# New constants for a planner's transfer model, and a new table of due times, in a planned linear-attention and MLP-mixer kernel

## The chip, the cores and the metric

The kernel runs on one core of one Trainium2 chip. The metric is the device time of one execution in microseconds (us); for the kernel before it is given as the median of three runs. A profile is one further execution, recorded by the hardware profiler. TensorE is written PE, VectorE DVE, ScalarE ACT, GpSimd POOL, and SyncE SP.

## The reference, cut to what matters

Two branches start from the same normalised rows; one gates the other, and the input is added. S is 2048 rows, D is 512, F is 1376, and attention has 32 heads of 16.

```
x  = A_x
xn = layernorm(x)
s  = A(xn)                    # linear attention
g  = silu(B(xn))              # mixer and MLP
return x + s * g

A: q, k, v = split(xn @ wqkv); phi(t) = where(t > 0, t + 1, exp(t)) + 1e-6
   kv = sum_s phi(k) v^T;  z = sum_s phi(k)
   o  = phi(q) kv / (phi(q) z + 1e-6);  A = o @ wo
B: h  = gelu(layernorm(xn) @ w1); its four column groups shifted by +1, -1, +2, -2 rows
   x1 = xn + shifted(h) @ w2
   B  = x1 + gelu(layernorm(x1) @ w3) @ w4
```

## The kernel before, in words

The rows are cut into 16 tiles of 128, four to a block, so that there are four blocks of 512 rows. Each product is made from rounded halves (names ending in `h` and `l`): three matmuls stand for one exact one. The work runs in this order: keys and queries of the four blocks with the running Gram sums (`k`, `q`, `pax`, `pbx`, `pex`, `g`), the first mixer product (`h`), the second (`pam`, `pbm`, `pem`), the up-projection (`a`, `pa`, `pb`, `pe`) with attention between its parts (`pas`, `pbs`, `pes`), and the down-projection (`acc` for block 0, `pad`, `pbd`, `ped` for blocks 2, 3 and 1).

No instruction is issued where the program text names it. The text builds a list of 5542 operations (`Plan.add`, with a duration, the tiles read and written and, for a transfer, its megabytes `mb`). `Plan.emit` then goes through simulated time: it picks the next operation of each engine, gives it its buffers and issues it. What it picks is set by

- the due time of each operation: matmuls get theirs from a nominal sequence (`deadlines`), all others one that leads back from what they feed (`backward`);
- the table `SOONER`, pairs of an operation's number and a whole number k: `nudged` moves that operation's due time earlier by 0.25 us times k (later where k is negative), and then carries the change back to what feeds it;
- the simulated time at which its inputs are there and its buffers are free. For PE an operation may be taken out of turn only when its nominal place lies at most 9 us behind that of the first one not yet done (`window=9.0`).

Transfers are simulated as one queue, `dma`, the time at which the last transfer leaves it. Ordinary transfers (loads, stores and fetches) are issued from SP; adding transfers (`gather`, the form in which the transfer adds to what lies in SBUF) are issued from POOL, `soft` in the code. At most eight of each kind are simulated as under way (`under`). For a transfer issued at time `s`, `op.end` is the simulated time of landing, from which its readers and the free buffers are counted. Each engine runs what it was given in the order of issue, and semaphores guard the data, so a wrong estimate costs waiting and nothing else.

The places that the prediction speaks of: a block's rows are read and their statistics made (`load_rows`, `totals`); `spread(b)` makes from them four numbers per row, which PE turns, ACT copies (`ar`) and SP stores to two rows in HBM (`arow`, `nrow`); `load_u(b, 1)` loads the transposed input in four parts (`xt`, 128x512 f32, 0.262 MB each) and adds the row `nrow` to each by an adding transfer; each part is then rounded by ACT (`u_ch`) and its rest made by DVE (`u_cl`), and these feed the products of `pair_kq`. `phi_k` adds each key tile to `zacc` by an adding transfer, `mix2` adds the normalised rows (`o<-xnd`), `gate` adds the input (`th<-in_x`).

Of the kernel before, what the change touches and what calls it, by code (L numbers as in the profile page):

```python
# [85 lines left out]
class Plan:  # L86
# [183 lines left out]
    def emit(self, first, lead, reserve, window, ahead, table=()):  # L270
# [13 lines left out]
        port, dma = 0.0, 0.8  # L284
# [6 lines left out]
        while left:  # L291
# [5 lines left out]
            for e, cands in avail.items():  # L297
                picks = []
                low = INF
                for op in cands:  # L300
                    s = max(free[e], op.ready)
                    if op.mb:
                        s = max(s, under[e == "POOL"][0] + self.GAP)
                    if op.two and s < port:
                        s = port
                    if e == "POOL" and not op.mb and not op.two:
                        s = next((b + .02 for a, b in lock if a <= s < b), s)
                    if op.table is not None and op.table != table:
                        s = max(s, free[e] + 1.28)
                    ok = True  # L310
                    fresh = [t for t in op.tiles if t.ap is None]
                    for t in fresh:
# [7 lines left out]
                        s = max(s, q[need - 1][0] + (self.GAP if e != "PE" else self.PE_GAP))  # L320
# [24 lines left out]
            s, op = best  # L345
# [13 lines left out]
            op.end = s + op.lat * k  # L359
            if op.mb:  # L360
                soft = e == "POOL"
                late = min(.92, 1.03 * max(0.0, dma - s))
                dma = max(dma, s + (.97 if soft else .06)) + op.mb * (4.59 if soft else 3.43)
                op.end = max(dma + (1.89 if soft else 1.29) + late, s + (4.08 if soft else 2.08 if op.loads else 2.2))
                under[soft].pop(0)
                under[soft].append(op.end)
            if op.two:
# [29 lines left out]
def linear_attn_gated_by_mixer(  # L397
# [1398 lines left out]
    for b in LINE:  # L1796
# [9 lines left out]
        down_late(b, final)  # L1806

    SOONER = (
# [48 lines left out]
    )  # L1857
    pl.emit(first=6.0, lead={"p": 9.0, "w": 20.0, "ab": 10.0}, reserve={"p": 8, "w": 1, "ab": 0}, window=9.0,
            ahead=6.0, table=SOONER)
# [39 lines left out]
```

## Time and profile before

| | us |
|---|---|
| median of 3 runs (lowest, highest) | 503.36 (502.1, 504.45) |
| the profiled execution, its own time | 506.13 |
| its span, first to last instruction's end | 504.4 |
| PE busy | 495.1 |
| DVE busy | 436.9 |
| ACT busy | 370.6 |
| POOL busy | 124.1 |

The page of the profile gives busy time by engine, shares in 40 slices, the queues of the transfers, and the chain of work that ended last. Other views answer for a part: waits (which engine waited for whose instruction), a table by stretches of time (busy time of each engine with the number of its instructions, the granted clock of PE, the share of the transfer engines that was busy and the GB/s), one tile's instructions, and the chain of waits in order of time. A busy time of PE is taken from start to modelled end, and matmuls overlap; the number of matmuls in a stretch tells more than its busy time.

### The profile page before, as it was taken

How to read it: one execution, taken by the hardware profiler on the slowest of the kernel's cores; microseconds unless marked ns; L12 is line 12 of the kernel's file. 1: busy time of each engine (PE TensorE's matmuls, PEld its weight loads, DVE VectorE, ACT ScalarE, POOL GpSimd, SP SyncE). 2: the span in 40 equal slices, each digit the busy share in tenths (PEclk: the TensorE clock that was granted, in tenths of full speed). 3: DMA queues.
4: the chain of work that ended last, by engine and by line, in shares of the span. 5: the costliest groups of instructions: out<-in, count | busy, mean ns of one | idle time of the engine just before them, and what ended most of it. 6: DMA issues, size and time to landing. Idle time of an engine off the chain costs nothing.

```text
span 504.4 us, 9873 instructions
## 1 busy us (share of the span) xinstructions
PE 495.1 (98%) x3240; PEld 446.8 (89%) x3240; DVE 436.9 (87%) x869; ACT 370.6 (73%) x840; POOL 124.1 (25%) x214
## 2 busy tenths in 40 slices
PE   8999979999999999999999999999999999999996
PEld 5788857777788988799988989999999999999996
DVE  4998768699889967999899999999999789795973
ACT  5897979976768669999996757765676676664631
POOL 1384601717950213042210021100000000144330
PEclk9999999999999999999999999999999999999999
DMA  7869895799994699979985789986443789689996
GB/s 218 304 168 230 218 261 139 177 280 275 301 324 102 181 282 305 293 206 259 344 278 196 231 187 265 254 278 185 145 126 106 239 277 329 175 163 291 297 249 177
DMA packets 87083, 117.44 MB, mean 233 GB/s; under 512 B 10328, under 2 KB 39160, under 8 KB 87032
## 3 DMA queue, kind: packets, MB, share of 16 engines
q1 hardware_dynamic: 75512, 96.11, 58.4%
q0 software_dynamic: 11520, 20.71, 24.1%
q8 instruction: 25, 0.41, 0.4%
q14 instruction: 26, 0.21, 0.1%
HBM read 72.66 MB, written 39.93 MB: 223 GB/s over the span
## 4 chain that ended last, share of the span: by engine, by line
PE 89%; DMA 5%; DVE 3%; ACT 2%; SPq 1%; issue 0%; DVEq 0%; ACTq 0%
PE pb L146 9%; PE pbd L146 9%; PE h L146 9%; PE g L146 8%; PE acc L146 6%; PE pbx L146 5%; PE pe L146 5%; PE pbm L146 5%; PE ped L146 5%; PE pbs L146 4%; PE q L146 3%; PE k L146 3%; PE pex L146 3%; PE pad L146 3%; PE pem L146 2%; PE pa L146 2%
## 5 line engine op out<-in xcount | busy, mean ns | idle before, releaser
L225 POOL DMA_DIRECT2D xo<-x1d x12 | 10.8, 948 | 160.5 <-ACT d_a11xh L168 110.9
L225 POOL DMA_DIRECT2D o<-xnd x16 | 14.0, 894 | 48.9 <-ACT o L168 19.1
L225 POOL DMA_DIRECT2D th<-in_x x14 | 12.3, 905 | 38.4 <-DVE th L201 23.2
L225 POOL DMA_DIRECT2D zacc<-ke x12 | 11.9, 991 | 31.6 <-DVE xf L191 21.8
L168 ACT ACTIVATE th<-xo 128x512 f32<-128x512 f32 (+1 forms) x16 | 9.5, 611 | 11.4 <-DVE xo L201 10.1
L225 POOL DMA_DIRECT2D xt<-nrow x16 | 14.9, 1373 | 7.4 <-DMA nrow<-ar 4.2
L168 ACT ACTIVATE ht<-ht 128x512 f32<-128x512 f32 x16 | 9.8, 626 | 6.7 <-DVE ht L191 6.7
L191 DVE TENSOR_TENSOR ht<-h,abc 128x512 f32<-128x512 f32 x16 | 10.9, 685 | 4.4 <-PE h L146 4.0
L168 ACT ACTIVATE p<-pb 128x256 f32<-128x256 f32 x20 | 7.6, 382 | 9.1 <-PE pb L146 8.9
L196 POOL TENSOR_SCALAR w<-mv 128x4 f32<-128x4 f32 (+2 forms) x10 | 4.4, 440 | 36.0 <-ACT sq L168 35.6
L168 ACT ACTIVATE y<-o,nm,rs 128x512 f32<-128x512 f32 x16 | 12.0, 806 | 0.5 <-POOL nm L196 0.5
L168 ACT ACTIVATE sq<-o,mv 128x512 f32<-128x512 f32 x16 | 11.5, 721 | 0.1
L168 ACT ACTIVATE p<-pe 128x256 f32<-128x256 f32 x20 | 7.7, 383 | 5.2 <-PE pe L146 4.8
L201 DVE SCALAR_TENSOR_TENSOR pq<-pq,rd 128x512 f32<-128x512 f32 x16 | 10.8, 680 | 0.2
L201 DVE SCALAR_TENSOR_TENSOR qz<-pq,zb 128x512 f32<-128x512 f32 x16 | 10.8, 679 | 0.0
L1456 DVE TENSOR_REDUCE den<-qz 128x32 f32<-128x512 f32 x16 | 10.7, 679 | 0.1
L598 POOL TENSOR_TENSOR rs<-w,nhalf 128x4 f32<-128x4 f32 (+2 forms) x10 | 10.2, 1020 | 0.7
L168 ACT ACTIVATE sq<-o 128x512 f32<-128x512 f32 x16 | 9.9, 625 | 0.0
L168 ACT ACTIVATE u<-pb 128x256 f32<-128x256 f32 x20 | 7.7, 383 | 3.1 <-PE pb L146 2.8
L168 ACT ACTIVATE x<-x,nm,rs 128x512 f32<-128x512 f32 x12 | 9.0, 805 | 0.0
L201 DVE SCALAR_TENSOR_TENSOR th<-th,so 128x512 f32<-128x512 f32 x12 | 8.1, 680 | 0.6 <-ACT th L168 0.5
L168 ACT ACTIVATE sq<-x,mv 128x512 f32<-128x512 f32 x12 | 8.5, 710 | 0.0
(2043 smaller groups left out, 2435.2 us busy)
## 6 DMA issues: line engine op xcount, KB each, us to landing
w_s<-in_w SPq DMA_DIRECT2D x28, 256.0 KB
x<-in_x SPq DMA_DIRECT2D x16, 256.0 KB
xt<-in_xt SPq DMA_DIRECT2D x16, 256.0 KB
xnd<-x SPq DMA_DIRECT2D x16, 256.0 KB
xt<-nrow POOLq DMA_DIRECT2D x16, 256.0 KB, 7.9
pqd<-qr SPq DMA_DIRECT2D x16, 256.0 KB
o<-xnd POOLq DMA_DIRECT2D x16, 256.0 KB, 7.1
x1d<-o SPq DMA_DIRECT2D x16, 256.0 KB
```

Of the source, the lines that this page charges most:

```text
L146: lambda: nc.tensor.matmul(out.get(), lhs.get(), rhs.get(), start=start, stop=stop, skip_group_check=more))
L168: nc.scalar.activation(out.get(), src.get(), func, scale=get(scale), **kw)
L191: self.vec(eng, out, [a, b], lambda: self.e(eng).tensor_tensor(out.get(), a.get(), b.get(), op=op), True)
L196: lambda: self.e(eng).tensor_scalar(out.get(), a.get(), get(s1), get(s2), **kw), False,
L201: lambda: self.nc.vector.scalar_tensor_tensor(out.get(), a.get(), get(s), b.get(), op0=op0, op1=op1),
L225: lambda: self.nc.gpsimd.dma_start(out.get(), get(src), accum_op=ALU.add), mb=mb)
L598: lambda: g.tensor_tensor(out.get(), src.get(), nh.get(), op=ALU.pow))
L1456: pl.add("DVE", .6, .68, [t], [den], lambda: nc.vector.tensor_reduce(den.get(), t.get().rearrange("p (h d) -> p h d", d=DH), axis=AX.X, op ...
```

## The change

The list of operations, their sizes, tiles and dependences stay as they are. Changed are the constants by which `Plan.emit` simulates a transfer, and the whole table `SOONER`. In the simulation an ordinary transfer takes 2.92 us per MB instead of 3.43, an adding one 4.93 instead of 4.59; the time from issue to entering the queue, from leaving it to landing, and the shortest time from issue to landing change as well, and the part of the delay `late` that grows with the queue grows by half. A load and a store no longer differ in their shortest time. The old table has 490 pairs, the new one 565; 197 operations stand in both, 56 of them with the same number.

```diff
             if op.mb:
                 soft = e == "POOL"
-                late = min(.92, 1.03 * max(0.0, dma - s))
-                dma = max(dma, s + (.97 if soft else .06)) + op.mb * (4.59 if soft else 3.43)
-                op.end = max(dma + (1.89 if soft else 1.29) + late, s + (4.08 if soft else 2.08 if op.loads else 2.2))
+                late = min(1.38, 1.54 * max(0.0, dma - s))
+                dma = max(dma, s + (.66 if soft else .39)) + op.mb * (4.93 if soft else 2.92)
+                op.end = max(dma + (2.12 if soft else 1.46) + late, s + (3.02 if soft else 2.21))
                 under[soft].pop(0)
                 under[soft].append(op.end)
...
     SOONER = (
-        23, 8, 39, 7, 48, -50, 69, 53, 90, 10, 93, 21, 96, 20, 97, 12, 99, 9, 106, -6, 118, -9, 120, 6, 124, 8,
...
-        -29, 5428, -15, 5478, -18, 5486, -12, 5493, 8, 5514, 38, 5519, -24,
+        23, 13, 37, 5, 41, 2, 47, -18, 48, -112, 52, -101, 54, 3, 60, 2, 72, 7, 92, -38, 95, -17, 96, 48, 100,
...
+        5373, -5, 5379, 30, 5380, -25, 5392, 17, 5419, 19, 5422, -29, 5478, -30, 5493, 13, 5513, 18,
     )
```

99 rows, old and new, of the table SOONER are left out of this document.

## The prediction, made before the result was known

> **What bounds the kernel now.** I read the page first, for what is busy.
>
> ```profile
> span 504.4 us, 9873 instructions
> ## 1 busy us (share of the span) xinstructions
> PE 495.1 (98%) x3240; PEld 446.8 (89%) x3240; DVE 436.9 (87%) x869; ACT 370.6 (73%) x840; POOL 124.1 (25%) x214
> ```
>
> PE is busy for 98% of the span, but matmuls overlap in these records, so I went on to the table by stretches, which counts them. Columns: stretch, its length, then busy us and (number) of PE, weight loads, DVE, ACT and POOL, then PE's granted clock, the busy share of the transfer engines, GB/s.
>
> ```profile
> 60.00:65.00 5.00, 5.00 (x24) 4.03 (x23) 4.40 (x8) 5.00 (x10) 3.37 (x4) 1.00 0.90 236
> 65.00:70.00 5.00, 5.00 (x23) 4.09 (x22) 3.19 (x6) 3.45 (x6) 0.00 (x0) 1.00 1.11 204
> 70.00:75.00 5.00, 2.21 (x7) 1.20 (x7) 2.95 (x8) 3.06 (x6) 0.00 (x0) 0.93 1.02 327
> 75.00:80.00 5.00, 5.00 (x18) 3.97 (x17) 4.13 (x8) 4.10 (x8) 0.87 (x1) 0.73 0.74 179
> 80.00:90.00 10.00, 10.00 (x44) 8.00 (x44) 7.22 (x12) 10.00 (x26) 2.58 (x5) 1.00 0.44 129
> 80.00:180.00 100.00, 100.00 (x470) 81.46 (x470) 88.50 (x168) 77.80 (x154) 43.81 (x95) 1.00 0.82 225
> 180.00:300.00 120.00, 120.00 (x800) 108.90 (x799) 108.56 (x220) 102.58 (x254) 23.09 (x34) 1.00 0.91 259
> 300.00:500.00 200.00, 199.65 (x1674) 198.63 (x1673) 175.21 (x362) 124.86 (x301) 25.18 (x29) 1.00 0.80 223
> 500.00:504.40 4.40, 0.40 (x4) 0.19 (x2) 1.54 (x3) 0.38 (x1) 0.00 (x0) 0.99 0.45 165
> ```
>
> From 80 to 500 us PE is idle for 420 - (100.00 + 120.00 + 199.65) = 0.35 us. An order can give nothing back there; it can only lose. Between 70 and 80 us stand 7 + 18 = 25 matmuls where a steady ten microseconds hold 44: 19 are missing, and at 10/44 = 0.227 us each that is **4.3 us lost**. The waits of PE name the cause (columns: who waited for whom, us in total, times, the longest):
>
> ```profile
> PE pax L146 <- DVE u_2l L191: 2.3, 1, 2.3
> PE warm L146 <- POOL ones L514: 1.0, 1, 1.0
> PE k L146 <- ACT u_1h L168: 0.8, 1, 0.8
> PE pax L146 <- ACT u_2h L168: 0.5, 1, 0.5
> PE k L146 <- DVE wk_1l L191: 0.3, 1, 0.3
> ```
>
> The pair of projections that opens block 2 waits for the third part of its input, 0.5 us for the half `u_2h` and 2.3 us for `u_2l`: 2.8 us. The other 4.3 - 2.8 = 1.5 us are a slower clock behind the wait:
>
> ```profile
> 72.00:74.00 2.00, 0.00 (x0) 0.00 (x0) 1.53 (x4) 1.03 (x2) 0.00 (x0) 1.00 1.05 387
> 74.00:76.00 2.00, 1.78 (x4) 1.48 (x5) 2.00 (x6) 1.82 (x5) 0.87 (x1) 0.57 0.50 191
> 76.00:78.00 2.00, 2.00 (x7) 1.52 (x6) 2.00 (x5) 1.70 (x4) 0.00 (x0) 0.58 0.78 137
> ```
>
> From 74 to 78 us 11 matmuls ran at a granted 0.57 and 0.58, where 4/0.227 = 17.6 would fit: 6.6 x 0.227 = 1.5 us, as the remainder says. The view of the tile `xt` in 50 to 80 us shows why the data were late (times of the first and last start stand behind the durations):
>
> ```profile
> L225 POOL DMA_DIRECT2D xt<-nrow x4: 864/1387/1711, 58.9 to 60.8; - x4
> L168 ACT ACTIVATE u_0h<-xt x1: 615/615/615, 66.5 to 66.5; 128x512 fp32r<-128x512 f32 x1
> L168 ACT ACTIVATE u_3h<-xt x1: 630/630/630, 72.5 to 72.5; 128x512 fp32r<-128x512 f32 x1
> DMA to landing us min/median/max: 6.8/9.5/11.7
> ```
>
> Four adding transfers are issued between 58.9 and 60.8 us; the reader of the first starts at 66.5, that of the last at 72.5. They land (72.5 - 66.5)/3 = 2.0 us apart, the slowest 11.7 us after its issue.
>
> **The change part by part.** *The operations.* Nothing is added or removed: the same 3240 matmul records, the same transfers. Cost 0. What the constants cost on the chip is 0 too; they act through the order alone.
>
> *How well the new constants fit.* The queues, with their share of the 16 transfer engines over the span:
>
> ```profile
> q1 hardware_dynamic: 75512, 96.11, 58.4%
> q0 software_dynamic: 11520, 20.71, 24.1%
> ```
>
> Ordinary: 0.584 x 504.4 / 96.11 = 3.06 us per MB; the old 3.43 is 12% too slow, the new 2.92 5% too fast. Adding: 0.241 x 504.4 / 20.71 = 5.87; the old 4.59 is 22% too fast, the new 4.93 16%. Both move towards the trace. That speaks for a truer plan, with one warning: the side of the error for ordinary transfers changes, from cushion to shortage.
>
> *The stall of block 2.* With the issue times of before, the simulated landing of the last `xt` part moves by: 0.262 MB x (4.93 - 4.59) = 0.09 us for each adding transfer, 0.45 for four and the `zacc` one among them; 2.12 - 1.89 = 0.23 behind the queue; at most 1.38 - 0.92 = 0.46 of `late`; 0.66 - 0.97 = -0.31 ahead of it. The sum is +0.8 us. So the new plan sees a gap of 0.262 x 4.93 = 1.29 us between two adding transfers instead of 1.20, where the trace has 2.0. It has a reason to bring this chain forward by 0.8 us, not by the whole wait of 2.8. Bounds: 0, if the new order leaves the chain where it is, and 2.8, if it happens to be early enough. I take 0.8, which the constants give. PE cannot fill much of the hole with later work: it may reach only 9 us ahead, and a pair is 42 matmuls, 9.5 us. What is late next is the fourth part, one gap of 2.0 us behind the third and read by the same product.
>
> *The clock behind it.* A wait of 2.0 us in place of 2.8 leaves the 1.5 us somewhere between all paid and none. Nothing here shows a wait of that length, so 0 to 1.5 saved; I take 0.5, nearer to the one row there is. The Trainium skill ("TensorE: Matmul & The Clock Gate", "What's actually happening") says that the clock halves after an idle window of about 3.4 us. The trace disagrees in the length: here it fell to 0.57 after a longest wait of 2.3 us. By the rule a shortened wait would cost no clock at all and the saving would be 0.8 + 1.5 = 2.3 us, which would be 501.1.
>
> *The start.* The first waits, 1.0, 0.8 and 0.3 us, follow the first loads and constants. The table touches early operations (47, 48 and 52 make the key weights' halves), so up to 2.1 us can go and about as much can come. I take 0, since nothing queues ahead of the first loads.
>
> *80 to 500 us.* 0 to gain. I take 0, and what can be lost is the second rival.
>
> *The end.* The chain of waits ends so (start, us, what):
>
> ```profile
> 498.14 2.27 PE pbd L146 x19
> 500.44 0.39 ACT th L168
> 500.86 0.44 DVE th L201
> 501.31 0.42 DVE th L191
> ```
>
> Behind the last matmul are three operations and one store, 504.4 - 500.4 = 4.0 us. The order of these is forced by data; another store just ahead would cost 0.262 x 3.06 = 0.8 us, or save it. I take 0.
>
> **The sum:** -0.8 - 0.5 = -1.3 us. The profiled execution took 506.13 us for its span of 504.4 and lies 2.77 us above the median of 503.36; its span would become 503.1 and its time 504.8. From the median: 503.36 - 1.3 = **502.1 us**.
>
> **The rivals.** *The stall goes altogether.* The whole order in front of it is made anew, with 75 pairs more in the table, and the chain of statistics, `nrow`, `xt` and `u` has many places to win two microseconds: the store of `nrow` alone kept POOL waiting 4.2 us.
>
> ```profile
> POOL xt L225 <- DMA nrow<-ar: 4.2, 1, 4.2
> ```
>
> Against it: the constants ask for 0.8 only. It gives 503.36 - 4.3 = 499.1.
>
> *A new wait in the late stages, slower.* The chain of waits runs through stores and fetches where PE does not stop yet, and one stage is full of ordinary transfers:
>
> ```profile
> 399.97 2.05 DMA wf_b211h<-w4d
> 405.67 6.43 DMA wt<-wt_40h
> 400.00:425.00 25.00, 24.90 (x210) 24.68 (x209) 23.00 (x48) 18.66 (x44) 0.00 (x0) 1.00 0.90 291
> ```
>
> In these 25 us 291 GB/s are 7.28 MB. The old plan counts 25.0 us for them, the new one 21.2, the trace has 0.90 x 25 = 22.5. A plan that holds the queue to be 3.7 us shorter may issue fetches that much later or put other transfers ahead; if the cushion was all there was, PE waits 3.7 us and pays the 1.5 us of slow clock. That is +5.2, and with the forecast's -1.3 it gives 503.36 + 3.9 = 507.3. It decides once a fetch or the store of 6.43 us lands later than PE needs it by over 1.3 + 2.5 = 3.8 us, clock included. For it: PE idles 0.10 us there already. Against it: the old 11% of cushion is spread over many transfers, and DVE and ACT have idle time to catch up.
>
> *The change does not do what it says.* If adding and ordinary transfers share the engines, no single queue with fixed rates says when one lands, and the stall stays, perhaps at another place: 503.4, between 501.5 and 505.5. The row for 65 to 70 us speaks for it: share 1.11 and only 204 GB/s, against 387 GB/s at 1.05 in 72 to 74. The Trainium skill ("DMA: Bandwidth & Descriptors", "Queues, rings and completion order") says that each transfer engine goes round between the queues that have work, a packet at a time. By that rule an adding transfer is slowed by ordinary ones issued after it, which this plan cannot count; the gap of 2.0 us against its 1.29 agrees.
>
> **How the numbers follow.** The forecast, a stall that is shortened, has a chance of 0.33; the stall gone 0.32; the new wait 0.29; the case in which the change does not do what it says 0.06. About 0.5% (2.5 us) is what a measurement here tells from no change. The forecast and the third rival are within it: 0.39 together. The stall gone is faster by more: 0.32. The new wait is slower: 0.29. The forecast's own range is 501.1 to 503.4, from the clock fully saved to no gain. For 8 in 10: the low end is 499.1 less 0.6 of the start's 2.1, 498.5; the high end 507.3 and a store's 0.8 at the end, 508.1.
>
> **What the profile of after would show.** The table by stretches: the stretch with fewer than 44 matmuls in 10 us, between 65 and 85; 21 missing or more means no gain, under 5 the first rival. The waits of PE: `pax` for `u_2l`, near 1.5 us by the forecast. A wait of PE over 1 us for a `wf`, `wu`, `yt` or `d_` tile after 180 us, and a granted clock below 0.9 behind it, is the second rival. It would be wrong in its ground if PE's matmul counts between 80 and 180, 180 and 300 or 300 and 500 us changed by over 10 with no wait named, or if the time outside the span moved by over 1 us.

## The result, and the profile after

The changed kernel takes 508.05 us (median of 9 executions, 506.06 to 509.75) against 503.36 us for the kernel before (median of 9, 501.08 to 506.47): a ratio of 1.0071, 95% interval 1.0045 to 1.0097. It is slower, by about 0.7% in this comparison. The unaltered pair was run side by side twice more: 507.16 against 505.90 (1.0013, 0.9991 to 1.0036) and 506.69 against 504.76 (1.0041, 1.0012 to 1.0070). All three ratios lie over 1, two of them clear of 1; the loss is small, some 0.4% or 2 us, and single executions scatter by more than that. The intervals of the first two do not even meet, so ratios of different sets of runs that lie half a per cent apart say little. So below an edit is judged first by the stretch of the profile that it touches, and only then by its time.

The profiled execution of the changed kernel took 509.00 us for a span of 507.0; the time outside the span went from 1.7 to 2.0 us, which is 0.3 us of the loss. From the page of the changed kernel:

```profile
span 507.0 us, 9889 instructions
...
PE 494.8 (98%) x3240; PEld 445.2 (88%) x3240; DVE 436.3 (86%) x869; ACT 372.2 (73%) x840; POOL 127.9 (25%) x214
...
q1 hardware_dynamic: 75512, 96.11, 58.3%
q0 software_dynamic: 11520, 20.71, 24.3%
```

The work is the same: the same transfers, bytes and matmul records. The table by stretches, first one row of the kernel before, then the changed kernel (columns as in the prediction):

```profile
70.00:80.00 10.00, 7.21 (x23) 5.16 (x23) 7.09 (x15) 7.16 (x13) 0.87 (x1) 0.83 0.88 253
```

```profile
70.00:80.00 10.00, 10.00 (x44) 7.72 (x43) 9.16 (x19) 9.17 (x17) 0.86 (x1) 1.00 1.07 340
80.00:180.00 100.00, 99.98 (x473) 81.82 (x471) 87.68 (x166) 76.50 (x151) 44.05 (x94) 1.00 0.82 224
180.00:300.00 120.00, 120.00 (x806) 109.20 (x805) 109.18 (x220) 103.18 (x254) 23.12 (x35) 1.00 0.88 251
300.00:500.00 200.00, 196.02 (x1640) 194.65 (x1640) 172.08 (x356) 123.65 (x297) 24.69 (x28) 1.00 0.82 225
```

The stall of block 2 is gone: 44 matmuls between 70 and 80 us where there were 23, and no slow clock. But from 300 to 500 us there are 1640 instead of 1674. The waits of PE say where new holes are:

```profile
PE pb L146 <- ACT u L168: 2.4, 2, 1.2
PE ab L151 <- POOL an L196: 2.0, 1, 2.0
PE ped L146 <- DVE d_s11l L191: 1.6, 1, 1.6
PE warm L146 <- POOL ones L514: 1.1, 1, 1.1
```

To place them, the same stretches of both kernels, first the kernel before, then the changed one:

```profile
30.00:40.00 10.00, 10.00 (x45) 7.98 (x44) 9.18 (x16) 7.75 (x17) 9.43 (x13) 1.00 0.84 201
310.00:330.00 20.00, 20.00 (x171) 20.00 (x171) 19.90 (x43) 15.16 (x40) 1.72 (x2) 1.00 0.97 280
470.00:480.00 10.00, 10.00 (x87) 10.00 (x86) 9.74 (x19) 6.83 (x14) 4.37 (x5) 1.00 1.10 294
```

```profile
30.00:40.00 10.00, 7.97 (x35) 6.14 (x34) 7.98 (x13) 6.45 (x12) 9.58 (x12) 1.00 0.59 150
310.00:330.00 20.00, 17.59 (x143) 16.90 (x142) 16.82 (x37) 11.97 (x33) 1.75 (x2) 1.00 0.98 249
470.00:480.00 10.00, 8.43 (x72) 8.22 (x71) 7.97 (x16) 6.79 (x14) 3.53 (x4) 1.00 1.05 263
```

Counted in matmuls at the rate of the full rows: 21 more in block 2 at 10/44 us are 4.8 us won; 10 fewer at 30 to 40 us are 2.3 lost; 28 fewer at 310 to 330, at 20/171 us, are 3.3 lost; 15 fewer at 470 to 480, at 10/87, are 1.7 lost. The balance of these four is a loss of 2.5 us; the spans differ by 2.6. That they agree so well is in part luck, since smaller differences remain: 5 fewer in the rest of 20 to 60 us, 9 more from 180 to 300, 15 more from 330 to 470. The rows from 0 to 300 us, of the kernel before and of the changed one, show that the changed kernel is still ahead there, by 13 matmuls, in spite of the hole at 34 us:

```profile
0.00:300.00 300.00, 295.07 (x1566) 247.94 (x1567) 260.15 (x505) 245.32 (x539) 98.91 (x185) 0.99 0.86 240
```

```profile
0.00:300.00 300.00, 295.78 (x1579) 247.84 (x1580) 260.81 (x507) 247.17 (x542) 103.17 (x186) 1.00 0.85 239
```

What decides is behind 300 us. How each hole comes about:

*At 34 us.* PE's transposition `ab` of block 1 waits for POOL's small operations on the statistics. Their rows in the kernel before and in the changed one (start, us, engine, what):

```profile
29.57 0.53 POOL L196 TENSOR_SCALAR pu<-mv 128x4 f32<-128x4 f32 x1 [0.62 <-DVE mv L587]
30.19 1.37 POOL L598 TENSOR_TENSOR an<-pu,nhalf 128x4 f32<-128x4 f32 x1
```

```profile
29.53 3.39 POOL L196 TENSOR_SCALAR pu<-mv 128x4 f32<-128x4 f32 x1 [0.49 <-DVE mv L587]
33.01 1.48 POOL L598 TENSOR_TENSOR an<-pu,nhalf 128x4 f32<-128x4 f32 x1
```

The same 128x4 operation starts at the same time and takes 3.39 us instead of 0.53. Beside it DVE runs a train of operations that read two operands in SBUF, each starting before the one ahead has ended:

```profile
29.77 0.69 DVE L191 TENSOR_TENSOR x1l<-x,x1h 128x512 fp32r<-128x512 f32 x1
30.38 1.29 DVE L201 SCALAR_TENSOR_TENSOR kr<-kt,kr 128x512 f32<-128x512 f32 x2
31.58 0.69 DVE L191 TENSOR_TENSOR x2l<-x,x2h 128x512 fp32r<-128x512 f32 x1
32.18 0.69 DVE L191 TENSOR_TENSOR kq_f<-wk_s,wq_s 128x512 f32<-128x512 f32 x1
32.91 0.69 DVE L201 SCALAR_TENSOR_TENSOR kq_f<-kq_f,wq_s 128x512 f32<-128x512 f32 x1
```

The last one reads what the fourth writes and starts only when that is through (32.18 + 0.69 = 32.87); POOL's operation ends at 29.53 + 3.39 = 32.92, just there. The hole belongs to the new table: with it and the old constants (e8) PE waits 2.4 us for `ab`, with the old table and the new constants (e11) 0.6.

*At 316 and 323 us.* ACT takes its work in order, and ahead of the copies `u` that PE needs stand the rounding of `q4t` and the copy of `q5t`. Both wait for a fetch:

```profile
316.56 0.63 ACT L168 ACTIVATE q4h<-q4t 128x512 fp32r<-128x512 f32 x1 [2.91 <-DMA q4t<-q4d]
...
323.83 0.42 ACT L168 ACTIVATE q<-q5t 128x256 fp32r<-128x256 f32 x1 [2.11 <-DMA q5t<-q5d]
```

In the kernel before `q4h` ran at 316.30 with no wait. The four fetches of `q4t` (64 KB each) were issued from 307.5 to 310.2 us. The trace shows the landing of the first two, at 315.9 and 316.1, 8.4 and 8.0 us after their issue.

If I put the issue times of the trace into the new constants, the four land at 312.4 to 312.9, over 3 us too early. The old constants give 312.5 to 313.0, nearly the same. So at this place the exchange of the constants did not make the estimate worse. From 300 to 350 us the kernel before has 422 matmuls and the changed kernel 390; the new table with the old constants (e8) has 396, the old table with the new constants (e11) 409. By these single profiles most of this loss comes with the new table.

*At 477 us.* ACT's `d_s21h` waits until an output store gives its buffer back, and holds `d_s11h` behind it:

```profile
474.15 0.63 ACT L168 ACTIVATE d_s21h<-d1f_s21f 128x512 fp32r<-128x512 f32 x1 [2.63 <-DMA out<-th]
```

### The profile page after: what moved, and what is told of

Same layout as the page of the kernel before. It is cut to its first block, busy times and chain, and to the rows that moved or that the text cites. A ratio compares the mean times of both kernels' runs of the same rounds, so it can differ in the third digit from the quotient of the medians.

```text
span 507.0 us, 9889 instructions
## 1 busy us (share of the span) xinstructions
PE 494.8 (98%) x3240; PEld 445.2 (88%) x3240; DVE 436.3 (86%) x869; ACT 372.2 (73%) x840; POOL 127.9 (25%) x214
## 3 DMA queue, kind: packets, MB, share of 16 engines
q1 hardware_dynamic: 75512, 96.11, 58.3%
## 4 chain that ended last, share of the span: by engine, by line
PE 81%; DMA 9%; DVE 4%; ACT 2%; POOL 1%; SPq 1%; issue 1%; DVEq 0%; ACTq 0%
PE pb L146 10%; PE h L146 9%; PE pbd L146 7%; PE g L146 7%; PE acc L146 6%; PE pbx L146 6%; PE pe L146 5%; PE pbm L146 4%; PE pbs L146 4%; DMA out<-th 4%; PE ped L146 3%; PE pex L146 3%; PE pa L146 3%; PE pem L146 2%; PE a L146 2%; PE pes L146 2%
## 5 line engine op out<-in xcount | busy, mean ns | idle before, releaser
L201 DVE SCALAR_TENSOR_TENSOR qr<-qe,qi 128x512 f32<-128x512 f32 x11 | 7.5, 685 | 1.8 <-ACT qe L168 1.8
```

The costliest lines, as they stand in the source:

```text
L201: lambda: self.nc.vector.scalar_tensor_tensor(out.get(), a.get(), get(s), b.get(), op0=op0, op1=op1),
```

## The experiments

Theory A: the loss is the sum of these few waits, each made by an operation that stands in an in-order queue behind something that comes later than the planner counts. Rival B: the waits only show what was late first, and time saved at one of them is waited out at the next. Further rivals are named with their runs. "Ratio" is to the kernel before in the same set of runs (its medians were 505.42, 505.90, 504.85, 504.28 and 504.76 us in the five sets, in the order of time).

| run | us | ratio, 95% interval |
|---|---|---|
| e1_q4_behind | 508.13 | 1.0053 (1.0023, 1.0083) |
| e2_pu_on_dve | 506.04 | 1.0011 (0.9988, 1.0034) |
| e3_late_store | 506.90 | 1.0037 (1.0010, 1.0063) |
| e4_all_three | 505.94 | 1.0014 (0.9987, 1.0042) |
| e5_after_again | 507.16 | 1.0013 (0.9991, 1.0036) |
| e6_gaps_in_dve | 506.42 | 1.0024 (0.9994, 1.0055) |
| e7_no_adding_at_306 | 504.88 | 0.9983 (0.9958, 1.0009) |
| e8_new_table_old_constants | 510.22 | 1.0084 (1.0055, 1.0113) |
| e9_fetch_by_due | 506.90 | 1.0044 (1.0018, 1.0071) |
| e10_gaps_fetch_store | 506.16 | 1.0018 (0.9999, 1.0038) |
| e11_old_table_new_constants | 508.63 | 1.0090 (1.0064, 1.0115) |
| e12_before_again | 506.92 | one execution |
| e13_adding_after_fetch | 507.28 | 1.0054 (1.0019, 1.0090) |
| e14_after_third | 509.00 | 1.0088 (1.0053, 1.0122) |
| e15_no_table_old_constants | 515.22 | 1.0193 (1.0137, 1.0249) |
| e16_no_table_new_constants | 520.06 | 1.0312 (1.0242, 1.0383) |
| e17_after_once_more | 506.69 | 1.0041 (1.0012, 1.0070) |
| e18_no_table_ordinary_new | 517.61 | 1.0259 (1.0194, 1.0324) |

### The unaltered kernels again: e5, e17, e12

> The changed kernel once more, unaltered, as the base for the runs beside it. Theory A (its new waits belong to its order, not to one execution): the profile shows again about 2 us for the transpose ab behind POOL, 2 to 3 us for u in the stretch of 310 to 330 us, 1 to 2 us for the operands of ped, and no wait for pax; 0.4 to 1.0% slower than the kernel before. Rival (the losses of the first profile were of that execution): other waits in other places, and a ratio whose interval holds 1.

> The unaltered changed kernel beside the unaltered kernel before, a third time. Theory A (the change is a loss of some 0.4%, the mean of the two comparisons so far): ratio 1.002 to 1.007. Rival H (the first comparison was an outlier, there is no difference): ratio 0.998 to 1.002.

> The kernel before, unaltered, for a second profile of its stall in block 2. Theory A (the stall belongs to its order): again a wait for pax of 2 to 3 us between 70 and 80 us, 22 to 30 matmuls in that stretch, and a clock under 0.7 behind it. Rival G (the first profile of before, at 506.13 us against a median of 503.36, fell on an execution with a long stall, and it varies): a wait of less than 1.5 us there and over 36 matmuls.

In both new profiles of the changed kernel PE waits 2.0 us for `ab`, and 2.4 and 2.2 us for `u`; between 310 and 330 us it is busy 17.59 and 17.77 us, as in the first (17.59). Those two belong to the order. The wait for `d_s11l` does not: 0.2 us in e5, none in e17. The kernel before shows its stall again, shorter, with a wait of 1.8 us for `u_2l`:

```profile
70.00:80.00 10.00, 8.21 (x29) 5.93 (x28) 7.53 (x16) 7.98 (x14) 0.86 (x1) 0.83 1.00 276
```

With 29 matmuls it loses 15 x 10/44 = 3.4 us there. Both profiles of the kernel before (506.13 and 506.92 us) are of executions above its medians, so what the stall costs in a usual one is not shown. Of the two ratios one lies in the interval of theory A and one in that of rival H; the three together speak for about 0.4%.

### The hole at 34 us: e2 and e6

e2 gives `pu<-mv` of block 1 to DVE, at its place in the order:

```diff
         pl.ts(p, var(mv1, b * QT, b * QT + QT), kv * (1.0 + EPS), EPS * EPS, ALU.mult, ALU.add, eng="POOL")
+        if b == 1:
+            v = var(mv1, b * QT, b * QT + QT)
+            pl.ops[-1].emit = lambda: nc.vector.tensor_scalar(
+                p.get(), v.get(), kv * (1.0 + EPS), EPS * EPS, op0=ALU.mult, op1=ALU.add)
```

> The changed kernel, but the small operation pu<-mv of block 1 (128x4, 3.39 us on POOL in the profile after, 0.53 in the profile before) is given to DVE at the same place of the order; nothing else is moved. Theory A: the wait of PE for the transpose ab (2.2 us lost at 32.4) goes for the most part, since the power behind it still runs on POOL; the time falls by 1.2 to 2.2 us, to about 506.3. Rival B: the power operation or the other POOL operations of the group are stretched beside DVE instead, or the next operand is late, and the time falls by less than 0.6 us.

The wait for `ab` stays at 1.6 us. POOL's next operation is stretched instead, from 1.48 us to

```profile
30.37 3.20 POOL L598 TENSOR_TENSOR an<-pu,nhalf 128x4 f32<-128x4 f32 x1 [1.59 <-DVE pu L624]
```

So it is the place that stretches, not the operation: rival B. The ratio of e2, 1.0011, is that of the unaltered changed kernel in e5 (1.0013).

e6 leaves POOL as it is and opens DVE's train, by two small operations that read what the one ahead has written:

```diff
+            if op.order in (170, 154):
+                t = next(t for t in op.tiles if t.name in ("kr2", "kr3"))
+                self.nc.vector.tensor_scalar(self.junk, t.ap[:, :4], 1.0, 0.0, op0=ALU.mult, op1=ALU.add)
             op.at = s
...
+    pl.junk = fixed("junk", QT).ap
```

> The changed kernel with two small operations more on DVE (128x4, about 0.15 us each), one behind each of the two operations kr<-kt,kr that run beside POOL's pu<-mv at 30 us; each reads what the operation ahead of it wrote, so that DVE starts it only when that one is through. Theory A1 (POOL's small operations get at SBUF only where DVE's train of operations with two SBUF inputs has a gap; the train has none from 29.8 to 32.9): pu ends at about 31 instead of 32.9, the power behind it by 32.7, the wait for ab shrinks from 2.0 to under 0.7, and the time falls by 1 to 2 us against the changed kernel run beside it. Rival B1 (POOL is held by something else that ends at about 33, such as its own gather's descriptors): pu or the power still ends at 33 or later, and the wait for ab stays at 1.6 or more.

The rows of DVE and of POOL in e6:

```profile
30.06 0.69 DVE L201 SCALAR_TENSOR_TENSOR kr<-kt,kr 128x512 f32<-128x512 f32 x1
30.78 0.17 DVE L358 TENSOR_SCALAR junk<-kr 128x4 f32<-128x4 f32 x1
...
31.58 0.17 DVE L358 TENSOR_SCALAR junk<-kr 128x4 f32<-128x4 f32 x1
```

```profile
29.21 1.59 POOL L196 TENSOR_SCALAR pu<-mv 128x4 f32<-128x4 f32 x1 [0.49 <-DVE mv L591]
30.88 1.55 POOL L602 TENSOR_TENSOR an<-pu,nhalf 128x4 f32<-128x4 f32 x1
```

`pu` ends at 30.80, in the first gap (30.75 to 30.78), and the power at 32.43, when it had the second: theory A1. The wait for `ab` falls from 2.0 to 0.7 us and the stretch of 30 to 40 us holds 42 matmuls instead of 35. The Trainium skill ("SBUF — State Buffer", "Who interferes with whom") says that a DVE instruction with two SBUF inputs contends with a GpSimd instruction that reads SBUF, and that the shared port pair is an exclusive lock. The trace agrees, with 3.39 us for an operation of 0.53. Yet the time fell by 0.7 us only. One reason: from 0 to 80 us e6 has 308 matmuls and the changed kernel 304, so of the 7 gained at 30 to 40 us only 4 are left at 80. PE comes to block 2 earlier (its first product there starts at 70.99 us instead of 71.98) and finds the data less ready. Here rival B is half right.

### The hole at 310 to 330 us: e1, e9, e7, e13, e14

e1 lets ACT give out `q4h` and `q5` behind the `u` that PE waits for. Some operations are held back until another has been given out; the plan itself is not touched:

```diff
-            op.emit()
+            if op.order in HELD:
+                held.setdefault(HELD[op.order], []).append(op)
+            else:
+                op.emit()
+                for o in held.pop(op.order, ()):
+                    o.emit()
...
+HELD = {3284: 3179, 3286: 3231}
```

> The changed kernel, but ACT gives out q4h after u21_2 instead of ahead of it, and q5 after u21_3; everything else stands as in the changed kernel. Theory A (the loss is the sum of a few new waits, each made by an operation that stands in an in-order queue behind a transfer which lands later than planned): the waits of PE for u (1.31 us at 316.1 and 1.40 us at 323.2 in the profile after) go, and the time falls by 2.0 to 2.7 us, to about 505.7. Rival B (the waits of PE only show what was late first, the next operand is late by as much): other waits of PE come in the next 10 us, and the time falls by less than 0.7 us, to over 507.3.

e9 does the same to SP: the four fetches of `q4t` go ahead of two of `y_1t` and one of `pq` (`HELD = {3353: 3271, 3354: 3271, 3519: 3271}`).

> The changed kernel, but the four fetches of q4t are issued ahead of three other fetches (two of y_1t, 128 KB each, and one of pq, 256 KB) that the order gives out just before them and whose data are used later; all work is kept, no other engine's order is touched. Theory A (the late landing of q4t alone makes the waits of 316 and 323 us): q4t is issued 1 us earlier and lands about 2 us earlier, at 313.5 to 314.5; ACT's wait for it (2.9 us after) falls under 1.3, PE is busy for 18.6 us or more of 310 to 330 (17.6 after), and the time falls by 1 to 2.4 us against the changed kernel (507.16 beside a kernel before of 505.9). Rival C (the engines are shared with the adding transfers, so that the fetches gain nothing from their place in the queue): landing less than 0.7 us earlier, PE at 18 us or less in that stretch.

e7 leaves out the two adding transfers that run beside the exchange:

```diff
             pl.gather(th, x[i * P:(i + 1) * P, :])
+            if i < 2:
+                pl.ops[-1].emit = lambda: None
```

> The changed kernel without the two adding transfers th<-in_x of the first two row blocks (issued at 304.1 and 306.0 us in the profile after, 256 KB each): their share of the sum, the input added to the output, is left out of those 256 rows. Theory A (the fetches of q4t land at 316 instead of the 312.5 of the fitted rates, since they share the engines with adding transfers, and ACT's queue and with it PE wait for that): q4t lands 1.5 us or more earlier, ACT's wait for it shrinks from 2.9 to under 1.4, and PE is busy for over 18.8 of the 20 us from 310 to 330, where it was 17.6; 1 to 2.5 us less in all. Rival C (the small packets of the fetches alone make them late, the adding ones do not matter): q4t lands less than 0.7 us earlier and PE's share of that stretch stays within 0.5 us of 17.6.

e13 and e14 keep all work; the second adding transfer waits for `q4t`, by a small operation of POOL that reads it, and its store goes behind the fetches of `q5t` (`HELD = {2916: 3271, 2917: 3281}`). e14 has this alone (its label misnames it), e13 also the gaps of e6 and the store of e3.

> On the changed kernel: the two small operations on DVE at 30 us, the late store told to the planner, and the second adding transfer th<-in_x (306 us) starts only when q4t has landed, by a small operation of POOL that reads q4t ahead of it; its output store goes behind the fetches of q5t. All work is kept. Theory A (the adding transfer beside the exchange is what makes q4t late): PE is busy for over 19 of the 20 us from 310 to 330 (17.6 after, 18.5 in the run with the fetches moved), and the three places give 2 + 1.4 + 0.8 us, a time of 502 to 504.5, 0.2 to 0.7% faster than the kernel before beside it. Rival B (what is put off comes back: the store or the next adding transfers make q5t late instead): PE under 18.6 in that stretch, the time within 1 us of the run with the fetches moved (506.2 against 504.85).

> The changed kernel with the second adding transfer alone put behind the landing of q4t and its store behind the fetches of q5t, none of the other edits. Theory A: PE busy for over 19 us of 310 to 330, and 1 to 2.4 us less than the changed kernel, a ratio to the kernel before of 0.997 to 1.003. Rival B: PE under 18.6 there, ratio 1.003 or more.

The stretch of 310 to 330 us in e1, e9, e7 and e13, in this order:

```profile
310.00:330.00 20.00, 17.58 (x142) 16.74 (x141) 16.57 (x37) 11.90 (x32) 1.74 (x2) 1.00 0.88 228
```

```profile
310.00:330.00 20.00, 17.24 (x141) 16.61 (x140) 16.46 (x36) 12.29 (x32) 1.74 (x2) 1.00 0.93 248
```

```profile
310.00:330.00 20.00, 20.00 (x170) 19.93 (x169) 19.81 (x43) 14.53 (x36) 1.74 (x2) 1.00 0.94 274
```

```profile
310.00:330.00 20.00, 18.67 (x154) 18.15 (x153) 18.01 (x40) 12.92 (x33) 3.06 (x4) 1.00 0.90 239
```

A new order on ACT removes the two waits of the first profile and gives others of the same sum, for `p` and `h_a211f`: 17.58, rival B. New places for the fetches bring `q4t` in earlier (6.2 us from issue to landing instead of 8.2; ACT's wait for it falls from 2.9 to 0.9), but then ACT waits 2.7 us for `q5t`: 17.24, theory A's figure missed. Putting the adding transfer off brings `q4t` in by 313.5 us in e13 and 315.0 in e14, and again `q5t` is late, by 2.2 us in e13 and 2.9 in e14. Taking work out of the queue fills the hole: e7 has 170 matmuls there, and is 2.3 us faster than the changed kernel run beside it, 0.3 of it outside the span. That alone would say that the transfers are too many for this stretch. But e6, which keeps all of them and has no edit here, has 170 as well in its profile:

```profile
310.00:330.00 20.00, 20.00 (x170) 19.88 (x169) 19.82 (x42) 14.21 (x37) 1.75 (x2) 1.00 0.96 277
```

Its fetches of `q4t` and `q5t` are issued earlier, from 306.1 and 315.8 us instead of 307.5 and 318.4; ACT waits 0.8 us for the one and not at all for the other. It does not get off free: PE waits 1.0 us for `u` before 305 us, and from 300 to 350 us e6 has 409 matmuls, between the changed kernel's 390 and the 422 of the kernel before. Still, the transfers can fit, so their sum does not explain the hole by itself. e10 and e13 contain the edit of e6 and have the hole again (152 and 154 matmuls). That PE waits here for data which hang on these fetches is shown; what decides when the fetches are issued and land stays open. The rate of the transfers in the changed kernel, and below it one row of e7:

```profile
305.00:307.00 2.00, 2.00 (x20) 2.00 (x19) 1.80 (x5) 1.66 (x6) 0.88 (x1) 1.00 1.15 298
307.00:312.00 5.00, 5.00 (x44) 5.00 (x43) 4.93 (x11) 3.87 (x10) 0.00 (x0) 1.00 1.24 203
316.00:319.00 3.00, 1.84 (x16) 1.64 (x15) 1.90 (x4) 2.31 (x7) 0.09 (x1) 1.00 0.98 370
```

```profile
307.00:312.00 5.00, 5.00 (x45) 5.00 (x44) 4.94 (x11) 3.84 (x11) 0.00 (x0) 1.00 1.14 202
```

Share of the engines divided by GB/s is the price, in the measure that gave the mean of 3.06: 1.15/0.298 = 3.9 us per MB at 305 to 307, where nearly all is ordinary fetches in small pieces; 1.24/0.203 = 6.1 at 307 to 312, where an adding transfer runs beside them; 0.98/0.370 = 2.6 at 316 to 319, where large rows are stored. The 6.1 is not the adding transfer's doing alone: in e7, with none under way, the same five microseconds cost 1.14/0.202 = 5.6. So ordinary transfers alone range from 2.6 to 5.6, and no one rate fits them. In e7 the second fetch of `q4t`, the last whose landing the trace shows, lands at 313.6 where the new constants give 310.7; in the changed kernel it is 316.1 against 312.9. Of an error of 3.2 us, 2.9 are there without the adding transfers. That the small pieces make it is likely and not tested by itself.

### The late store: e3

```diff
-                    insort(slots[t.tag], (t.end, t.slot))
+                    insort(slots[t.tag], (t.end + (3.2 if op.order == 4840 else 0.0), t.slot))
```

> The changed kernel, but the planner is told that the output store whose buffer d_s21h takes over gives the buffer back 3.2 us later than it counts (its lateness in the profile after); the order is the same up to that place (about 471 us) and differs in some 45 operations of 5526 behind it. Theory A (the landing's estimate alone makes this wait): ACT no longer waits 2.63 us for the store, the wait of PE for d_s11l (1.73 us) shrinks to the 0.5 us that the planner then shows itself, and the time falls by 0.6 to 1.2 us, to about 507.2. Rival B: the time stays within 0.4 us of the changed kernel's, since the tail waits for the same operands by another way.

ACT does not wait for the store, and no wait for `d_s11l` is left in the list. Since e5 and e17 hardly show this wait without any edit, it cannot be said what the edit is worth.

### Several edits together: e4 and e10

> The three edits of the other runs together. Theory A: the savings add up, 2.4 + 1.7 + 0.9 = 5.0 us less than the changed kernel, about 503.1, the level of the kernel before or a little under it. Rival B (the waits take each other's place): less than 2 us below the changed kernel, over 506.

> Three edits on the changed kernel together: the two small operations on DVE that let POOL in at 30 us, the four q4t fetches ahead of the three later ones, and the late store told to the planner. Theory A (the three places are independent): 1.4 + 1.6 + 0.8 = 3.8 us less than the changed kernel, about 1 to 3 us faster than the kernel before run beside it (ratio 0.994 to 0.998). Rival B (the time saved at one place is waited out at the next): within 1.5 us of the changed kernel, ratio 1.000 or more.

Both are within their interval of the kernel before and better than the changed kernel's first ratio, but neither beats the kernel before: 505.94 and 506.16 us, rival B in e10 by its ratio and in e4 within 0.1 us. In e10 310 to 330 us still has only 152 matmuls. No version here that does all the work is faster than the kernel before.

### Constants and table apart: e8, e11, e15, e16, e18

Without a table, `table=SOONER` is left out of the call of `emit`; otherwise only the three lines of constants are exchanged.

> The new table of shifts with the old constants, one part of the change alone. Theory D (table and constants fit only together: the table was made for an order that the planner gets with its own constants, and its own count for this crossing is 4.9 us longer than for the changed kernel): 3 to 8 us slower than the changed kernel, 511 to 516. Rival E (the constants are the harm, the cheap rate of the ordinary transfers takes the cushion, and the old ones give it back): within 1.5 us of the kernel before or faster than the changed kernel.

> The old table with the new constants, the other part of the change alone. Theory D (table and constants fit only together; the planner's own count for this crossing is 4.9 us longer than for the kernel before): 3 to 8 us slower than the kernel before. Rival F (the constants are the better part of the change and the new table the worse one): within 1.5 us of the kernel before, or faster.

> No table of shifts, old constants: the planner's own order. Theory D (the tables are worth far more than the constants: the planner's own count is 14 us longer without a table): 10 to 18 us slower than the kernel before, and the same within 1.5 us as the run without a table with the new constants, whose count is 507.4 against 507.5. Rival E (the new constants are worse in themselves): this one is faster than the other by over 2 us.

> No table of shifts, new constants. Theory D: 10 to 18 us slower than the kernel before, within 1.5 us of the run without a table with the old constants. Rival E: slower than that by over 2 us. Rival F (the new constants are better in themselves): faster than that by over 2 us.

> No table of shifts, the new constants for ordinary transfers, the old ones for adding transfers. The planner's own count for this order is 502.9 us, against 507.5 with the old and 507.4 with the new constants; the chip took 7.7 us more than the count with the old and 12.7 more with the new. Theory O (the ordinary transfers counted too cheap make the plan promise too much): again 11 to 14 us more than the count, 514 to 517. Theory P (the adding transfers' constants do): 6.5 to 9 us more, 509.4 to 512.

Crossed, each half of the change alone costs 0.8 to 0.9%: a table fits the constants it was made under (theory D). The planner's own count says so too, 4.9 us more for each crossing. With no table the new constants are worse than the old by 520.06 - 515.22 = 4.8 us, though the planner counts both orders equal (507.4 and 507.5): rival E, and theory D fails on this point. e18 names the half that does it. The chip exceeds the planner's count by 7.7 us with the old constants, 12.7 with the new, and 517.61 - 502.9 = 14.7 with only the ordinary ones new: theory O, even beyond its range. So without a table, ordinary transfers counted cheaper make a plan that the chip keeps less well.

With the tables this does not show. `Plan.emit` puts the end of the last matmul at 493.1 us for the kernel before and at 493.8 for the changed kernel, so the new plan is not even shorter by its own count. The chip exceeds the count, in one set of runs, by 12.9 us for the kernel before, 13.4 for the changed one and 11.5 for e8 with the old constants (510.22 against 498.7); in another by 11.8 for the kernel before and 10.7 for e11 with the new ones (508.63 against 497.9). The excess does not follow the constants there.

## Why the prediction was wrong, point by point

It gave 502.1 us (498.5 to 508.1), faster by 0.3%; the time is slower by 0.1 to 0.7%. The range held by 0.05 us in the first comparison, on the width that the second rival had given it; the sign did not.

*"80 to 500 us. 0 to gain. I take 0."* **This step failed.** It put the loss in the stretch without slack at nothing, though it said that an order "can only lose" there. 34 matmuls fewer from 300 to 500 us are about 4 us in the first profile (20 and 17 fewer in e5 and e17). It is a new wait in a late stage, as in the second rival, which had a chance of 0.29; place and price were off: not the weights at 400 us, where the changed kernel loses nothing, but the exchange of small pieces at 305 to 325; 3.3 us and no slow clock in place of 3.7 + 1.5. The rival's ground, a cheaper rate that uses up a cushion, is not shown here: the old constants put the landing of `q4t` as early as the new ones. Both were over 3 us short, in a stretch where ordinary transfers cost up to 5.6 us per MB against a mean of 3.06.

*"The stall of block 2 ... I take 0.8."* The size failed: the stall went altogether, as in the first rival. It was also larger than counted: in rows of 5 us a matmul that lies over their border counts twice, and in one row of 10 us the kernel before has 23 and not 25, so 21 are missing, 4.8 us. The reason given was wrong too. `u_2l` was late by its place in DVE's queue, not by the landing of its part, which ACT read at 70.30 us. DVE stood at an `xf` that waited for another part, with `u_2l` behind it (ACT's row, then DVE's, of the kernel before):

```profile
70.30 0.63 ACT L168 ACTIVATE u_2h<-xt 128x512 fp32r<-128x512 f32 x1 [0.72 <-DMA xt<-nrow]
...
72.47 0.42 DVE L191 TENSOR_TENSOR xf<-xt,xt 128x256 f32<-128x256 f32 x1 [1.75 <-DMA xt<-nrow]
...
73.49 0.68 DVE L191 TENSOR_TENSOR u_2l<-xt,u_2h 128x512 fp32r<-128x512 f32 x1
```

In the changed kernel `u_2l` comes right behind `u_2h`, ahead of the `xf`:

```profile
69.22 0.63 ACT L168 ACTIVATE u_2h<-xt 128x512 fp32r<-128x512 f32 x1 [0.27 <-DMA xt<-nrow]
...
69.88 0.69 DVE L191 TENSOR_TENSOR u_2l<-xt,u_2h 128x512 fp32r<-128x512 f32 x1 [0.21 <-ACT u_2h L168]
```

So the wait of 2.3 us for `u_2l` could go without any earlier landing. The four adding transfers are issued no earlier (59.5 to 61.3 us, before 58.9 to 60.8) and land as slowly (7.7 to 11.6 us). The third part is now used first (`u_2h` at 69.2 us, `u_0h` at 70.8); and PE begins the block's first product at 71.98 instead of 68.91 us, since it has already lost time at 34 us and does the Gram products first. "PE cannot fill much of the hole" was not so.

*"The clock behind it ... 0 to 1.5 saved; I take 0.5."* With no stall nothing was left to pay there. The sum also takes from the median a stall and a slow clock that were seen in an execution 2.8 us above it: of the 136 executions of the kernel before in the five later sets, 58 have a mean granted clock of 0.999 or more, so the slow clock is not paid every time. What a wait of 2.0 us costs the runs show at another place: see the last section.

*"How well the new constants fit."* The means are right: ordinary 0.583 x 507.0 / 96.11 = 3.08 us per MB after, adding 5.95. "That speaks for a truer plan" was not borne out. The warning was, in the runs without a table, by 5 to 7 us more over the planner's count; with the tables the excess does not show it. What the averages hide is that the rate of ordinary transfers alone differs by a factor of two from stretch to stretch. The row of 65 to 70 us that the prediction quoted for shared engines, 204 GB/s at a share of 1.11, is mostly adding transfers (0.80 of its 1.02 MB, at a share of 0.972: 0.972 x 5 / 0.80 = 6.1 us per MB, near their mean of 5.87). Its low rate needs no ordinary transfers beside them.

*"The start"* and *"the end"*, 0 each, hold in this profile: the first waits are 1.1 and 0.4 us twice, and behind the last matmul stand 4.0 us as before. The stretch from 20 to 60 us had no term at all, **and this failed as well**: 15 matmuls fewer there (160 instead of 175), some 3.4 us, were not foreseen, and POOL's stretched operations beside DVE were in the profile of before to be seen (1.37 us for `an<-pu,nhalf` at 30.19, where the next took 1.02).

## What to carry to other kernels

Where the bound engine has no idle time left, a new order can only win at its one stall and lose everywhere else, so sign and size hang on the stretches without slack: begin there. Before a wait is put down to a late transfer, see what stood ahead of the waiting operation in its engine's queue. Test a fitted rate stretch by stretch (share of the transfer engines over GB/s), not by its mean, and take a plan's own count as worth nothing until its excess on the chip has been measured with the same constants. Before one wait is edited away, ask what stands next in the same queue and when its data land: in each of the three ways tried here the wait moved to the next operand. And one profile that fills a hole does not prove the cause, as e6 beside e7 shows.

## What the runs showed of the hardware that I had not expected

A wait of PE of 1.97 to 2.03 us (the one for `ab`) stands in eight profiles of the changed kernel and of its variants. In four of them the clock fell behind it, in four it did not. The stretch behind it, in the changed kernel's first profile and in e5:

```profile
36.00:38.00 2.00, 2.00 (x10) 1.59 (x9) 1.32 (x3) 0.58 (x1) 1.83 (x5) 1.00 0.66 168
```

```profile
36.00:38.00 2.00, 2.00 (x6) 1.62 (x5) 0.94 (x2) 0.96 (x2) 1.92 (x4) 0.50 0.72 203
```

Six matmuls instead of ten, and over 30 to 40 us 29 instead of 35: 6 x 10/44 = 1.4 us more for the same wait, in one execution and not in the next. In the four that fell (e3, e5, e7, e14) PE had also waited 1.3 to 1.5 us for `u_1h` near 9 us, in the other four at most 1.2; whether the two hang together is not tested. In e10, where the wait for `ab` is 0.6 us, all twelve executions had a mean granted clock of 0.999 or more; but in e6 and e13, with 0.7 and 0.6 us, only nine and five of twelve had, so the shorter wait alone does not settle it. A small POOL operation can wait for a whole train of DVE operations (3.39 us for 0.53); why it got in between two of them in the kernel before, at 30.05 us, with no gap that the trace shows, stays open.
